# Gate and up in 128-token passes: four feature tiles to a PSUM tile instead of two, and the last 128 output rows cut 288 + 288 instead of 448 + 128

## The chip, the core and the metric

The kernel runs on one core of a Trainium2 chip. The metric is device time in microseconds (us) from start to end, lower is better. Single instructions are given in nanoseconds (ns). The engines are named as in the profile: PE (TensorE matmuls), PEld (its weight loads), DVE (VectorE), ACT (ScalarE), POOL (GpSimd) and SP (SyncE, which here only issues DMAs).

## What is computed

A transformer block of 2048 tokens with 576 features: a modulated layer norm, local attention in 32 heads (each token looks at itself and seven earlier tokens, two apart), a second modulated layer norm, and a gated MLP without a nonlinearity. All arrays are bfloat16. Cut to what matters:

```python
h = _layernorm(x) * (1 + ca) + sa
x = x + ga * attention(h, A_wqkv, A_wo)        # 8 keys per query, dilation 2
h = _layernorm(x) * (1 + cb) + sb
g = h @ w_gate                                  # 576 -> 4608
u = h @ w_up                                    # 576 -> 4608
x = x + gb * ((g * u) @ w_down)                 # 4608 -> 576
```

The six modulation rows come from `silu(c) @ w_mod`.

## The kernel before

**Chunks and passes.** The tokens are cut into ten chunks (`SIZES`, L34): four of 128 and six of 256. Attention works chunk by chunk (`project` and `attend`). Gate and up work in seven passes (`DOWN`, L36): four passes of 128 tokens (one chunk each), then three of 512 tokens (two chunks each). After the four 128-token passes, and after each 512-token pass, `down` multiplies 512 tokens by `w_down`.

**One pass of `gate_up` (L648).** The 4608 features are 36 tiles of 128, held as nine blocks of four (`FB`, L37). For each feature tile and each of gate and up there are five matmuls over the 576 input features: four *mains* with 128 rows (L679) and one *remainder* with the last 64 rows (L688). The gate remainder uses rows 0 to 63 of the array, the up remainder rows 64 to 127. A *unit* is what one PSUM tile of two banks holds: bank 0 is gate, bank 1 is up. In a 128-token pass a unit has two feature tiles (`nf`, L664), in a 512-token pass one. Three units make a group (`nu`, L705; there are three such PSUM tiles, `ps_mlp`, L101). A group runs in this order on PE: mains of unit 0, mains of unit 1, remainders of all three units in one burst, mains of unit 2. `evacuate` (L691) then has ACT copy a unit from PSUM to a bfloat16 tile `gu` (L697), and DVE multiply gate by up into `hh` (L701). There are two `gu` buffers. The PSUM of a unit is free for the next group when its ACT copy is done.

**What fills the time beside it.** Between the matmuls a `Pacer` (L775) runs the attention steps of the following chunk and the projection of the one after it, each at a fixed fraction of the pass. For the steps below: `turn` (L408) transposes the normalized tokens `xn` on PE; `modulate` (L427) writes `hT` from the two PSUM tiles turnA (three k-tiles, by DVE, L434) and turnB (two, by ACT, L436); `qk` (L472) multiplies `hT` by the query and key weights (`pq`, L485); the softmax subtracts on DVE (`dd`, L573), takes the exponential on ACT (L574), and DVE weights the shifted values (L611 to L614) into `o_sb`, which PE turns again and ACT copies to `oT` (L621, L622). Then come the output projection (`pw`, L628), the residual on DVE (`y`, L633), the second layer norm, and the value projection (`pv`, L510) with its ACT copies to `v_sb` (L514). The attention tiles share two PSUM banks (`ps_att`, L100).

**Order of the work.** Every engine runs its own instructions in order. For the four 128-token passes and their `down` the framework's scheduler decides that order from the program and its own estimates (`AUTO`, L38, L863). For the later passes PE keeps the program's order.

**Weights.** Blocks 2 to 5 stay in the space of `w_down` during the 128-token passes (`KEPT`, L46). The others go through three slots (`gwp`, L95). `block_done` (L333) asks for the next block's load when a block has been used: on POOL's queue in the first pass, later on SP's. Before the change it is called at the end of a group.

**The last rows.** `down` (L724) works through 128 tokens at a time with 36 matmuls for each of two halves of 288 columns, multiplies by `gb` (L742), adds the residual (L744) and stores. The last 128 rows are done in two parts, one after the other: 448 columns, then 128, each with its own store on SP.

Of the kernel before, what the change touches and what calls it, by code (L numbers as in the profile page):

```python
# [7 lines left out]
BF = mybir.dt.bfloat16  # L8
# [9 lines left out]
P = 128  # L18
D = 576
# [17 lines left out]
FB = 4  # L37
AUTO = 4  # L38
GU_BUFS = 3
NB = FT // FB  # L40

ORDER = [[0, 1, 2, 3, 4, 5, 6, 7, 8], [6, 7, 8, 5, 4, 3, 2, 1, 0], [8, 1, 0, 5, 4, 3, 2, 6, 7],
         [2, 0, 3, 6, 4, 5, 7, 1, 8], [7, 1, 8, 0, 2, 3, 4, 5, 6], [4, 5, 6, 0, 1, 2, 3, 7, 8],
         [3, 7, 8, 0, 1, 2, 4, 5, 6]]
# [19 lines left out]
def kernel(  # L64
# [13 lines left out]
    nc = tc.nc  # L78
    S = A_x.shape[1]
# [6 lines left out]
    def pool(name, bufs, **kw):  # L86
        return ctx.enter_context(tc.tile_pool(name=name, bufs=bufs, **kw))
# [11 lines left out]
    outp = pool("outp", 2)  # L99
# [3 lines left out]
    def att(shape, dt, name):  # L103
        return ps_att.tile(shape, dt, name=name, tag="att")

    def hp():
        return tc.high_priority()
# [11 lines left out]
    for sl, m0, off in ((slice(0, KT), 0, 0), (slice(KT, KT + 1), KT - 1, -64)):  # L119
        n = sl.stop - sl.start  # L120
# [10 lines left out]
    wd = wts.tile([P, FT, D], BF, name="wd")  # L131
# [18 lines left out]
    def load_x(ci, eng, js=None, behind=None):  # L150

        for j in range(SIZES[ci] // P) if js is None else js:
            xt = xin.tile([P, D], BF, name="x_t")
            if behind is not None:
                nc.vector.tensor_copy(xt[0:1, 0:1], behind)
            eng.dma_start(xt[:], x_flat[START[ci] + j * P:START[ci] + (j + 1) * P, :])
            x_tiles.setdefault(ci, []).append(xt)
# [167 lines left out]
    def load_next(ts=(0, 1), eng=nc.sync):  # L325
        if state["next"] < len(loads):
            load_gu(loads[state["next"]], ts, eng)
            state["next"] += 1

    def load_wd(f0, f1):  # L330
        nc.sync.dma_start(wd[:, f0:f1, :], B_w_down[f0 * P:f1 * P, :].rearrange("(k p) n -> p k n", p=P))

    def block_done(pi, b):  # L333
        if pi == KEPT_PASSES - 1 and b in KEPT:
            k = KEPT.index(b)
            load_wd(k * WDB, (k + 1) * WDB)
        for n in range(len(loads)):
            if last_use[n] == (pi, b) and n + GU_BUFS == state["next"]:
                load_next(eng=nc.gpsimd if pi == 0 else nc.sync)
        if (pi, b) == (0, ORDER[0][-2]):  # L340

            for cx in (4, 5):
                load_x(cx, nc.sync, behind=late["hh"][0:1, b * FB, 0:1])
            f0 = len(KEPT) * WDB
            nc.vector.tensor_copy(wd[0:1, f0, 0:1], late["hh"][0:1, b * FB, 0:1])
            load_wd(f0, FT)
# [301 lines left out]
    def gate_up(pi, c0, C, h2, step):  # L648

        hh = late["hh"]
        cs = slice(c0, c0 + C)
        ns = C / 2.4

        def tokens(rows, kt):
            return h2[rows, :, kt, :] if C > CH else h2[rows, c0 // CH, kt, c0 % CH:c0 % CH + C]

        def by_half(ap):  # L660
            return ap.rearrange("p (a c) -> p a c", c=CH) if C > CH else ap


        nf = 2 if C <= 256 else 1  # L664
        units = [(b, i) for b in ORDER[pi] for i in range(0, FB, nf)]

        def psum(k):

            if k < 3:
                t = ps_mlp.tile([P, 2, nf, 512 // nf], F32, name="pgu", tag="mlp")  # L670
                return [t[:, 0], t[:, 1]], t
            return [att([P, nf, 512 // nf], F32, "pgu" + "gu"[t])[:] for t in range(2)], None

        def main(u, first, beside=False):
            (b, i), out = units[u], ps[u][0]
            for n in range(nf):
                for t in range(2):
                    for kt in range(KT - 1):
                        nc.tensor.matmul(by_half(out[t][:, n, 0:C]), lhsT=gu_blocks[b][0][:, kt, t, (i + n) * P:(i + n + 1) * P], rhs=tokens(slice(0, P), kt),  # L679
                                         start=(first and n == 0 and kt == 0), stop=(not first and kt == KT - 2), skip_group_check=True)  # L680
                step(8 * ns, beside=beside if C > CH else None)

        def rem(u, first):
            (b, i), out = units[u], ps[u][0]
            for n in range(nf):
                for t in range(2):
                    rows = slice(64 * t, 64 * (t + 1))
                    nc.tensor.matmul(by_half(out[t][:, n, 0:C]), lhsT=gu_blocks[b][1][rows, (i + n) * P:(i + n + 1) * P], rhs=tokens(rows, KT - 1),  # L688
                                     start=(first and n == 0), stop=not first, skip_group_check=True)

        def evacuate(u):  # L691
            b, i = units[u]
            fs = slice(b * FB + i, b * FB + i + nf)
            with hp():
                g = late["gup"].tile([P, 2 * CM], BF, name="gu")[:, 0:2 * nf * C].rearrange("p (n t c) -> p n t c", n=nf, t=2)
                if ps[u][1] is not None:
                    nc.scalar.copy(g, ps[u][1][:, :, :, 0:C].rearrange("p t n c -> p n t c"))  # L697
                else:
                    for t in range(2):
                        nc.scalar.copy(g[:, :, t, :], ps[u][0][t][:, :, 0:C])  # L700
                nc.vector.tensor_tensor(hh[:, fs, cs], g[:, :, 0, :], g[:, :, 1, :], ALU.mult)  # L701

        nu = 4 if pi == len(passes) - 1 else 3  # L705
        ps, done = {}, 0
        for u in range(0, len(units), nu):
            for k in range(nu):
                ps[u + k] = psum(k)
                if k < 2:  # L710
                    main(u + k, True, k == 1)
            for k in range(nu):
                rem(u + k, k >= 2)
            step(2 * nu * nf * ns / 2)
            evacuate(u)
            evacuate(u + 1)
            for k in range(2, nu):
                main(u + k, False)
                evacuate(u + k)
            while done < NB and (done + 1) * FB <= (u + nu) * nf:  # L720
                block_done(pi, ORDER[pi][done])
                done += 1

    def down(di, r0, x_t, step):  # L724
        to_load = [(cx, j) for cx in LOAD_X_DOWN.get(di, []) for j in range(SIZES[cx] // P)]
        hh = late["hh"]
        for j in range(CM // P):

            cols = [(0, 448), (448, 128)] if r0 + (j + 1) * P == S else [(0, 288), (288, 288)]
            parts = [cols[0:1], cols[1:2]] if cols[0][1] != 288 else [cols]  # L730
            for part in parts:
                acc = ps_mlp.tile([P, 2, 512], F32, name="acc", tag="mlp")
                n, w, d0 = len(part), part[0][1], part[0][0]
                for f in range(FT):
                    for q, (q0, _) in enumerate(part):
                        nc.tensor.matmul(acc[:, q, 0:w], lhsT=hh[:, f, j * P:(j + 1) * P], rhs=wd[:, f, q0:q0 + w],  # L736
                                         start=(f == 0), stop=(f == FT - 1))
                    step(n * w / 2.4)
                with hp():
                    cs = slice(d0, d0 + n * w)  # L740
                    o_t = outp.tile([P, D], BF, name="y")[:, 0:n * w]
                    nc.vector.tensor_tensor(o_t.rearrange("p (n d) -> p n d", n=n), acc[:, 0:n, 0:w],  # L742
                                            gb_bc[:, cs].rearrange("p (n d) -> p n d", n=n), ALU.mult)
                    nc.vector.tensor_tensor(o_t, o_t, x_t[j][:, cs], ALU.add)  # L744
                (nc.gpsimd if n == 2 else nc.sync).dma_start(out_flat[r0 + j * P:r0 + (j + 1) * P, cs], o_t)  # L745
            if to_load:
                cx, jx = to_load.pop(0)
                load_x(cx, nc.gpsimd, [jx])
# [101 lines left out]
    def run_pass(pi):  # L850
        di, p = passes[pi]
        last = p is DOWN[di][-1]
        C = sum(SIZES[c] for c in p)
        total = FT * 9 * C / 2.4 + (FT * CM // P * 240 if last else 0)
        step = Pacer(passes[pi + 1][1] if pi + 1 < len(passes) else [], total)
        step(0)
        gate_up(pi, home[p[0]][1], C, h2T[di], step)
        if last:
            r0 = START[DOWN[di][0][0]]
            down(di, r0, [t for q in DOWN[di] for c in q for t in x_tiles[c]], step)  # L860
        step(0, rest=True)
# [36 lines left out]
```

## Time and profile before

| what | value |
|---|---|
| median of 4 runs | 574.71 us (574.07 to 575.86) |
| the profiled execution | 574.73 us, span 573.0 us |
| granted TensorE clock | 1.00 |
| four 128-token passes of gate and up, with the attention work beside them | 35.4 to 155.0 us of the span |
| last `down` of 512 rows | 534.1 us to the end |

The span goes from the first instruction to the last in the profile, and 1.7 us of the execution lie outside it. "Busy" is the time in which at least one instruction of the engine is open. PE's matmuls overlap in time, so PE counts as busy also where its matmuls start later than they could; such places show in the start times of neighbouring matmuls. In the views below a group of instructions is given as line, engine, operation, written tile <- read tiles, shape, count.

### The profile page before, as it was taken

The page shows a single profiled execution, that of the slowest core. Times are in us where ns is not written, and L with a number is a line of the kernel's source. Part 1 is how long each engine was busy: PE and PEld are TensorE (multiplying, and loading weights), DVE is VectorE, ACT ScalarE, POOL GpSimd, SP SyncE. Part 2 cuts the span into 40 slices and gives each one's busy share as a digit, 9 for nine tenths or more (in the row PEclk, how much of TensorE's full clock was granted, in tenths as well). Part 3 has the DMA queues.
Part 4 walks back from the last instruction along what each step waited for, and adds up shares of the span by engine and source line. Part 5 has one row for each costly group of instructions (what it writes and reads, how often), then busy time and mean ns, then how long its engine had stood idle before and what let it go on. Part 6 is the DMA issues. An engine that isn't in the chain of part 4 may idle for free.

```text
span 573.0 us, 12242 instructions
## 1 busy us (share of the span) xinstructions
PE 561.9 (98%) x5171; PEld 368.4 (64%) x5171; DVE 317.9 (55%) x695; ACT 222.2 (39%) x395; POOL 94.3 (16%) x165
## 2 busy tenths in 40 slices
PE   8899999999999999999999999999999999999997
PEld 4578898988878764554468764554457754444674
DVE  5778696868788775655394535744374422222201
ACT  3455565555602225445442005454440025444200
POOL 5462202020213211020501240011200110000000
PEclk9999999999999999999999999999999999999999
DMA  9999765259750345468402633476202214540000
GB/s 287 281 355 339 261 199 179 84 182 330 238 184 27 105 154 166 124 213 202 131 1 78 220 92 97 125 254 217 82 1 57 68 39 147 166 156 1 1 22 21
DMA packets 68457, 84.32 MB, mean 147 GB/s; under 512 B 19746, under 2 KB 59506, under 8 KB 68402
## 3 DMA queue, kind: packets, MB, share of 16 engines
q1 hardware_dynamic: 56738, 45.86, 27.2%
q0 software_dynamic: 9104, 34.44, 17.9%
q10 hardware_dynamic: 2560, 3.25, 1.7%
q8 instruction: 40, 0.66, 0.5%
q14 instruction: 15, 0.12, 0.1%
HBM read 70.93 MB, written 8.67 MB: 139 GB/s over the span
## 4 chain that ended last, share of the span: by engine, by line
PE 86%; DMA 8%; DVE 3%; ACT 1%; issue 1%; POOL 0%; ACTq 0%; DVEq 0%
PE pgu L679 38%; PE acc L736 24%; PE pgu L688 6%; PE pq L485 5%; DMA wd<-in_B_w_up_dram 4%; DMA wm<-in_w_mod_dram 4%; PE lgT L553 2%; PE pwB L628 2%; PE pwA L628 1%; PE pguu L679 1%; PE pgug L679 1%; PE pvA L510 1%; PE pvB L510 1%; PE warm L275 1%; DVE ln_stats L377 1%
## 5 line engine op out<-in xcount | busy, mean ns | idle before, releaser
L679 PE MATMUL pgu<-h2T,gm 128*128 128x512 bf16 (+1 forms) x1432 | 223.1, 308 | 1.1 <-ACT gu L697 0.7
L679 PEld LDWEIGHTS <-gm 128*128 128x128 bf16 x1504 | 119.0, 98 | 107.7 <-issue 14.2
L697 ACT CAST gu<-pgu 128x1024 bf16<-128x1024 f32 (+1 forms) x171 | 136.7, 835 | 130.1 <-PE pgu L688 103.6
L736 PE MATMUL acc<-wd,hh 128*128 128x288 bf16 (+2 forms) x1152 | 146.4, 286 | 0.0
L701 DVE TENSOR_TENSOR hh<-gu 128x512 bf16<-128x512 bf16 (+1 forms) x180 | 65.7, 370 | 127.6 <-ACT gu L697 118.5
L736 PEld LDWEIGHTS <-hh 128*128 128x128 bf16 x1152 | 110.9, 98 | 30.3 <-issue 0.4
L544 DVE TENSOR_TENSOR prod<-qT,kT 128x1280 bf16<-128x1280 bf16 (+1 forms) x80 | 47.0, 636 | 13.7 <-PE lgT L553 12.5
L527 POOL DMA_DIRECT2D vsh<-vd x30 | 22.7, 761 | 154.5 <-DMA vd<-v_sb 114.7
L745 POOL DMA_DIRECT2D out_dram<-y x15 | 8.5, 565 | 214.3 <-DVE y L744 214.3
L485 PE MATMUL pq<-hT,wqk 128*128 128x256 bf16 (+1 forms) x400 | 41.2, 251 | 0.8 <-DMA wqk<-in_A_wqkv_dram 0.8
L742 DVE TENSOR_TENSOR y<-acc,gb_bc 128x576 bf16<-128x576 f32 (+2 forms) x17 | 12.2, 718 | 51.8 <-PE acc L736 51.8
L611 DVE TENSOR_TENSOR vsh<-vsh,attn 128x2304 bf16<-128x2304 bf16 x30 | 39.9, 1352 | 0.2
L485 PEld LDWEIGHTS <-wqk 128*128 128x128 bf16 x400 | 32.3, 98 | 6.8 <-DMA wqk<-in_A_wqkv_dram 1.5
L679 PE MATMUL pgu<-h2T,wd 128*128 128x128 bf16 x512 | 34.9, 219 | 1.0 <-DMA wd<-in_B_w_up_dram 1.0
L688 PE MATMUL pgu<-h2T,gr 64*128 64x512 bf16 (+1 forms) x358 | 34.5, 307 | 0.0
L679 PEld LDWEIGHTS <-wd 128*128 128x128 bf16 x512 | 30.1, 98 | 2.9 <-DMA wd<-in_B_w_up_dram 1.5
L383 ACT ACTIVATE ln_rstd<-ln_stats,eps 128x2 f32<-128x2 f32 (+1 forms) x20 | 5.9, 296 | 66.4 <-DVE ln_stats L378 66.4
L377 DVE BATCH_NORM_STATS2 ln_stats<-x_t 128x6 f32<-128x288 bf16 x64 | 26.2, 447 | 1.8 <-DMA x_t<-in_A_x_dram 1.1
L688 PEld LDWEIGHTS <-gr 64*128 64x128 bf16 x376 | 12.5, 94 | 17.5 <-issue 10.6
L633 DVE TENSOR_TENSOR y<-pwA,ga_bc 128x288 bf16<-128x288 f32 x15 | 6.8, 456 | 26.1 <-PE pwA L628 25.9
L612 DVE TENSOR_TENSOR vsh<-vsh 128x2304 bf16<-128x2304 bf16 x15 | 20.3, 1352 | 0.0
L425 POOL TENSOR_SCALAR h2T<-h2T,modc 128x256 bf16<-128x256 bf16 x25 | 14.9, 604 | 30.0 <-DMA h2T<-xn_d 30.0
(153 smaller groups left out, 492.2 us busy)
## 6 DMA issues: line engine op xcount, KB each, us to landing
vsh<-vd POOLq DMA_DIRECT2D x30, 576.0 KB, 6.3
gm<-in_B_w_gate_dram SPq DMA_DIRECT2D x24, 512.0 KB, 3.9
gm<-in_B_w_up_dram SPq DMA_DIRECT2D x24, 512.0 KB, 5.0
wd<-in_B_w_down_dram SPq DMA_DIRECT2D x4, 1152.0 KB, 8.2
gm<-in_B_w_gate_dram POOLq DMA_DIRECT2D x5, 512.0 KB, 11.9
gm<-in_B_w_up_dram POOLq DMA_DIRECT2D x5, 512.0 KB, 11.7
out_dram<-y POOLq DMA_DIRECT2D x15, 144.0 KB, 2.1
wd<-in_B_w_gate_dram POOLq DMA_DIRECT2D x4, 512.0 KB, 10.1
```

The costliest lines, as they stand in the source:

```text
L377: nc.vector.bn_stats(stats[:, j, hf, :], src[j][:, hf * 288:(hf + 1) * 288])
L485: nc.tensor.matmul(pq[:, gi, 0:C], lhsT=wqk[:, kt, w0:w0 + P], rhs=h[:, kt, :], start=(kt == 0), stop=(kt == KT - 1))
L527: nc.gpsimd.dma_start(vsh[:].rearrange("p w d h -> p w (d h)"), src)
L544: nc.vector.tensor_tensor(prod[:, 0:nm, 0:C], qT[:, 0:nm, 0:C], kT[:, 0:nm, off:off + C], ALU.mult)
L611: nc.vector.tensor_tensor(vsh[:], vsh[:], attn[:, j, ws, None, :].to_broadcast([P, WG, DH, H]), ALU.mult)
L612: nc.vector.tensor_tensor(va[:], va[:], vb[:], ALU.add)
L628: nc.tensor.matmul(pw[q][:, 0:288], lhsT=oT[:, m, j * P:(j + 1) * P], rhs=wo[:, m, q * 288:(q + 1) * 288], start=(m == 0), stop=(m == KT - 1))
L679: nc.tensor.matmul(by_half(out[t][:, n, 0:C]), lhsT=gu_blocks[b][0][:, kt, t, (i + n) * P:(i + n + 1) * P], rhs=tokens(slice(0, P), kt), s ...
L688: nc.tensor.matmul(by_half(out[t][:, n, 0:C]), lhsT=gu_blocks[b][1][rows, (i + n) * P:(i + n + 1) * P], rhs=tokens(rows, KT - 1), start=(f ...
L697: nc.scalar.copy(g, ps[u][1][:, :, :, 0:C].rearrange("p t n c -> p n t c"))
L701: nc.vector.tensor_tensor(hh[:, fs, cs], g[:, :, 0, :], g[:, :, 1, :], ALU.mult)
L736: nc.tensor.matmul(acc[:, q, 0:w], lhsT=hh[:, f, j * P:(j + 1) * P], rhs=wd[:, f, q0:q0 + w], start=(f == 0), stop=(f == FT - 1))
```

## The change

In a 128-token pass a unit now has four feature tiles, one whole block: the two PSUM banks are filled to all 512 columns. A pass has 9 units in 3 groups instead of 18 in 6. `block_done` moves into the group, behind the evacuation of each unit after the first. And the last 128 rows are cut as 288 and 288 columns, still one part after the other. In the passes of 512 tokens a unit stays as it was.

```diff
-        nf = 2 if C <= 256 else 1
+        nf = min(FB, 512 // C)
...
             step(2 * nu * nf * ns / 2)
-            evacuate(u)
-            evacuate(u + 1)
-            for k in range(2, nu):
-                main(u + k, False)
+            for k in range(nu):
+                if k >= 2:
+                    main(u + k, False)
                 evacuate(u + k)
-            while done < NB and (done + 1) * FB <= (u + nu) * nf:
-                block_done(pi, ORDER[pi][done])
-                done += 1
+                while k > 0 and done < NB and (done + 1) * FB <= (u + k + 1) * nf:
+                    block_done(pi, ORDER[pi][done])
+                    done += 1
...
-            cols = [(0, 448), (448, 128)] if r0 + (j + 1) * P == S else [(0, 288), (288, 288)]
-            parts = [cols[0:1], cols[1:2]] if cols[0][1] != 288 else [cols]
-            for part in parts:
+            halves = [[0], [1]] if r0 + (j + 1) * P == S else [[0, 1]]
+            for qs in halves:
                 acc = ps_mlp.tile([P, 2, 512], F32, name="acc", tag="mlp")
...
```

The scheduler makes a new order of the four 128-token passes from it, on PE, ACT and DVE. On POOL the order stays. On SP a few weight loads change places. Behind these passes all queues keep their order.

More of the change, by code (lines that the diff above doesn't have):

```diff
@@ L727, in down @@
         for j in range(CM // P):
-            cols = [(0, 448), (448, 128)] if r0 + (j + 1) * P == S else [(0, 288), (288, 288)]
-            parts = [cols[0:1], cols[1:2]] if cols[0][1] != 288 else [cols]
-            for part in parts:
+            halves = [[0], [1]] if r0 + (j + 1) * P == S else [[0, 1]]
+            for qs in halves:
                 acc = ps_mlp.tile([P, 2, 512], F32, name="acc", tag="mlp")
-                n, w, d0 = len(part), part[0][1], part[0][0]
                 for f in range(FT):
-                    for q, (q0, _) in enumerate(part):
-                        nc.tensor.matmul(acc[:, q, 0:w], lhsT=hh[:, f, j * P:(j + 1) * P], rhs=wd[:, f, q0:q0 + w],
+                    for q in qs:
+                        nc.tensor.matmul(acc[:, q, 0:288], lhsT=hh[:, f, j * P:(j + 1) * P], rhs=wd[:, f, q * 288:(q + 1) * 288],
                                          start=(f == 0), stop=(f == FT - 1))
-                    step(n * w / 2.4)
+                    step(120 * len(qs))
                 with hp():
-                    cs = slice(d0, d0 + n * w)
-                    o_t = outp.tile([P, D], BF, name="y")[:, 0:n * w]
-                    nc.vector.tensor_tensor(o_t.rearrange("p (n d) -> p n d", n=n), acc[:, 0:n, 0:w],
+                    n, cs = len(qs), slice(qs[0] * 288, (qs[-1] + 1) * 288)
+                    o_t = outp.tile([P, D], BF, name="y")[:, 0:n * 288]
+                    nc.vector.tensor_tensor(o_t.rearrange("p (n d) -> p n d", n=n), acc[:, qs[0]:qs[-1] + 1, 0:288],
                                             gb_bc[:, cs].rearrange("p (n d) -> p n d", n=n), ALU.mult)
```

## The prediction

> **What bounds the kernel now.** I read the page first, then the chain of waits, then the timeline of the four 128-token passes, because only these passes and the last 128 rows change.
>
> ```profile
> PE 561.9 (98%) x5171; PEld 368.4 (64%) x5171; DVE 317.9 (55%) x695; ACT 222.2 (39%) x395; POOL 94.3 (16%) x165
> ...
> PE 86%; DMA 8%; DVE 3%; ACT 1%; issue 1%; POOL 0%; ACTq 0%; DVEq 0%
> ```
>
> PE is the bound, at full granted clock. Only two things can help: fewer or shorter steps of PE, and fewer places where PE's next matmul starts late. The table by stage gives PE 86.00 busy of 86.00 us from 207 to 293 us and likewise in the later passes, whose order stays as it is. So the change is worth what it does between 35 and 155 us, plus the tail.
>
> ```profile
> 31.33 9.21 DMA wd<-in_B_w_up_dram
> 40.83 13.12 DMA wd<-in_B_w_up_dram
> 53.99 0.84 PE pgu L679 x12
> ```
>
> These rows of the chain (start, length, what) show the first pass waiting for weights: block 5's up half lands at 40.83 + 13.12 = 53.95, and PE starts on it then. What PE saves before 53.95 is lost in this wait.
>
> ```profile
> 67.24 0.62 PE L679 MATMUL pgu<-h2T,gm 128*128 128x128 bf16 x8
> 67.79 0.51 PE L688 MATMUL pgu<-h2T,gr 64*128 64x128 bf16 x12
> ...
> 68.12 1.07 ACT L697 CAST gu<-pgu 128x512 bf16<-128x512 f32 x2 [1.99 <-PE pgu L688]
> 68.23 0.62 PE L679 MATMUL pgu<-h2T,gm 128*128 128x128 bf16 x8
> ```
>
> This is one burst of remainders. Mains follow each other at 56 ns (a row of 32 takes 1.79 us from start to start). Eight mains from 67.24 would end at 67.69, but the burst starts at 67.79. The twelve remainders are six gate-up pairs at 56 ns, 0.34 us, and would end at 68.13, but the next main starts at 68.23. So each burst costs 0.19 us beyond its matmuls. The first copy starts 0.33 us into the burst.
>
> **The change part by part.**
>
> 1. *Fewer bursts.* Matmuls and their lengths stay. Six bursts per pass become three. In passes 1 to 3 (counting from 0) nine bursts go: 9 x 0.19 = 1.7 us. In pass 0, after 53.95, three bursts become one, and twelve remainders that stood behind the wait now stand ahead of it, where PE has 0.7 us to spare: 2 x 0.19 + 0.34 = 0.7 us. **Sum -2.4 us.** The start times show 92 to 96 ns a side at every burst, so I hold this within 0.3.
>
>    The Trainium skill, "TensorE: Matmul & The Clock Gate", Part 3, The mechanism, says that a weight load overlaps a running matmul only when the two use different row groups. By that rule the load between two mains would be exposed as well and a burst would cost nothing extra; this term would be 0 and my sum 576.0. The rows above disagree: mains with 98 ns loads run at 56 ns, and only the change of row count costs.
>
> 2. *Old waits that go.* They are read from start times. Pass 1: turnB comes 0.34 late, because its PSUM bank is held until `dd` is done; mains at 89.49 come 0.61 late, since the unit's copy only ends then. Pass 2: the same two, 0.18 and 0.44. Pass 3: 0.31 for turnB and 0.20 for products. In the new order 24 remainders and 8 mains stand between the logits and the transposes instead of 16 mains (in pass 3 it is DVE's maximum that no longer queues behind a multiply), and the copy has 32 mains (1.79 us) to hide in instead of 16. **Sum -2.1 us**, bounds -1.0 and -2.1.
>
> 3. *New waits.* The copy becomes one of 1024 columns. Its length is in the passes of 512 tokens:
>
> ```profile
> L697 ACT CAST gu<-pgu 128x1024 bf16<-128x1024 f32 x99 | 96.9, 1015 | 107.6 <-PE pgu L688 87.3 <-PE pgu L679 8.6 <-DVE hh L701 6.2
> L697 ACT CAST gu<-pgu 128x512 bf16<-128x512 f32 x72 | 39.8, 588 | 22.6 <-PE pgu L688 16.3 <-DVE hh L701 3.0 <-PE pgu L679 1.6
> ```
>
>    Two copies of 588 become one of 1015: 36 x 0.161 = 5.8 us less of ACT, and DVE's multiply likewise (2 x 286 to 425 ns: 5.3 us less). Neither sets the end, so this is worth nothing by itself. But where a copy stands matters more. Now:
>
> ```profile
> 71.16 0.33 PE L414 MATMUL turnA<-identw,xn 128*128 128x128 bf16 x3
> ...
> 71.65 0.42 ACT L574 ACTIVATE dd<-dd 128x256 f32<-128x256 f32 x1 [1.15 <-DVE dd L573]
> ...
> 71.99 0.81 ACT L436 ACTIVATE hT<-turnB,modc 128x128 bf16<-128x128 bf16 x2
> ...
> 72.72 1.07 ACT L697 CAST gu<-pgu 128x512 bf16<-128x512 f32 x2
> ```
>
>    The exponential and ACT's half of `hT` come ahead of the two copies, and `pq` at 73.23 finds `hT` ready (72.80). In the new order ACT has: copy, copy, exponential, `hT`. Counted from the burst's start: the first copy waits for eight remainders instead of four, so 0.33 + 2 x 0.056 = 0.45. Two copies take about 0.91 each before the next can start, so the exponential starts at 2.27 and `hT` ends 1.15 later (71.65 to 72.80 above): 3.4. PE meanwhile needs 0.77 for the burst, 0.45 for 8 mains, 0.28 for five transposes, 1.0 for 18 mains: `pq` begins at 2.5 and needs ACT's k-tiles from 2.7. It loses **0.7 us** in pass 1. In pass 2 DVE writes its three k-tiles of `hT` (1.04 us) only behind the second multiply (2.4 + 0.4 = 2.8), so they are complete at 3.84: **0.8 us**. In pass 0 the same wait falls before 53.95 and costs nothing. In pass 3 the scheduler put the third copy there, with 24 mains to cover it: nothing.
>
>    Behind these stands the attention chain, later by some 0.9 us: in pass 1 `o_sb`, which had 0.4 us to spare (79.46 against 79.86), and the two banks of `pv` cost 0.1 each. In pass 2 DVE gets two multiplies of 0.4 instead of one of 0.2 between the products and `y`, so `pv`'s banks come free 0.46 late, the second `pv` and the transpose behind it wait 0.3 and 0.75 instead of 0.18 and 0.43: 0.9 more. In pass 3 the copies to `oT` stand behind a copy of twice the size: 0.4 more. **Sum +3.1 us** (0.9 + 1.7 + 0.5). Below, this is 0, if ACT's backlog is shorter than I add up; above I take twice it, 6 us, since the trace does not show this order.
>
>    A rule of the skill speaks against the change: "Perfetto Trace Analysis", Optimizing Scalar/DVE Operations, says that engines which are not saturated but cause bubbles elsewhere may do better with instructions broken up. ACT is 56% busy from 100 to 158 us, so the rule would have this term decide; without it the sum would be that of the first rival.
>
> 4. *Weights.* A group is three whole blocks, so without the moved `block_done` a slot would come back later. With it, a load waits for the mains of its block, as now. In pass 0 block 8's up half lands at 62.84, and PE needs it at 63.0 in the new order: 0.2 us of cover; if that is gone, the loss is as large as the lateness. Later loads land 5 us or more before use. 0, up to +0.5.
>
> 5. *The tail.* PE's time is equal: 36 x 189 + 36 x 56 = 8.8 us, and 72 x 122.5 = 8.8 us. What follows the last matmul grows:
>
> ```profile
> 567.58 0.62 DVE L742 TENSOR_TENSOR y<-acc,gb_bc 128x448 bf16<-128x448 f32 x1 [5.56 <-PE acc L736]
> 568.24 0.39 DVE L744 TENSOR_TENSOR y<-y,x_t 128x448 bf16<-128x448 bf16 x1
> ...
> 569.59 0.29 DVE L742 TENSOR_TENSOR y<-acc,gb_bc 128x128 bf16<-128x128 f32 x1 [0.96 <-PE acc L736]
> 569.91 0.23 DVE L744 TENSOR_TENSOR y<-y,x_t 128x128 bf16<-128x128 bf16 x1
> ```
>
>    Halfway between 128 and 448 columns lie 0.46 and 0.31: +0.17 and +0.08, and the last store is larger. **+0.3 us**, bounds +0.2 and +0.6.
>
> **Sum.** The profiled execution took 574.73 us (span 573.0 and 1.7 around it), the median is 574.71, so no shift between them. 574.73 - 2.4 - 2.1 + 3.1 + 0.3 = **573.6 us**.
>
> **Rivals.** About 0.3%, or 1.7 us, is what a measurement of this kernel can tell from no change: faster ends at 573.0, slower begins at 576.4.
>
> *The new waits don't come* (term 3 near 0). For it: ACT and DVE have 11 us less to do and PE has more cover per copy. Against it: the order on ACT is fixed, and two copies stand ahead of the exponential. 574.73 - 2.4 - 2.1 + 0.3 = 570.5 us. Chance 0.22.
>
> *The attention chain sets the pace of passes 1 to 3.* Its place is ACT between burst and exponential, its price the lateness of `hT`, `o_sb`, `y` and `v_sb` in turn. The chain has 0.4 us to spare at `o_sb`; beyond that each 0.1 us shows. With 0.9 at `hT`, 0.8 at `y` and 0.5 at `v_sb` a pass loses 2.2: 3 x 2.2 - 2.4 - 2.1 + 0.3 = +2.4, so 577.1 us. It decides from 1.4 us a pass (4.2 / 3). Against it: in pass 3 the third copy lies clear of the exponential. Chance 0.13.
>
> *The forecast*, 572.2 to 575.2 by itself: chance 0.65. A quarter of it lies below 573.0.
>
> Faster: 0.22 + 0.15 = 0.37. Slower: 0.13 and 0.02 of the forecast's upper end, 0.15. Same: 0.48. The range leaves out about one in ten on each side: 571.0 to 576.2.
>
> **What would show it.** Right: three bursts per pass on PE in the timeline, and 12 fewer of them; two copies of about 1.0 us ahead of the exponential; `pq` broken by a wait of 0.7 to 0.8 us in passes 1 and 2; the mains after a burst never late by ACT; the last multiply near 0.46 us. Wrong: `pq` without a gap (first rival), or `o_sb`, `pw` and `pv` waiting in every pass by 0.5 us or more (second), or mains of blocks 7 and 8 waiting for DMA.

## The result, and the profile after

The changed kernel takes **575.72 us** (median of 40 runs, 574.82 to 578.06); the kernel before took 574.92 beside it (58 runs). The ratio is 1.0015, 95% interval 1.0010 to 1.0020: 0.8 us slower, inside the forecast's range, but on the wrong side of no change. The profiled execution took 575.73 us, with a span of 574.0 at a granted clock of 0.998.

From the page of the changed kernel, the busy times, the shares of the chain that ended last, and ACT's copy:

```profile
PE 558.2 (97%) x5171; PEld 370.0 (64%) x5171; DVE 315.9 (55%) x659; ACT 217.3 (38%) x359; POOL 93.4 (16%) x165
...
PE 86%; DVE 5%; DMA 4%; ACT 2%; issue 1%; SPq 0%; POOL 0%; ACTq 0%; POOLq 0%; DVEq 0%
...
L697 ACT CAST gu<-pgu 128x1024 bf16<-128x1024 f32 x135 | 132.2, 1017 | 122.2 <-PE pgu L688 100.2
```

The change did what it says: 36 instructions fewer on ACT and on DVE, all copies are of 1024 columns, the same 5171 matmuls, and PE is busy 3.7 us less. The span is 1.0 us longer all the same, so PE must stand still for longer than it saved. Where, is read from the start times of the same places in PE's program (us; pass 3 runs up to the end of the first output projection `pw` behind it):

| stretch | before | after | difference | forecast |
|---|---|---|---|---|
| pass 0, together with its start | 65.34 | 64.91 | -0.43 | -0.7 |
| pass 1 | 27.37 | 27.05 | -0.32 | -0.6 |
| pass 2 | 31.58 | 31.60 | +0.02 | +0.5 |
| **pass 3** | **36.51** | **38.08** | **+1.57** | **-0.6** |
| rest of the first `down` | 46.79 | 46.55 | -0.24 | 0 |
| the 512-token passes and their `down` | 361.96 | 361.97 | 0 | 0 |
| last matmul to the end | 3.44 | 3.81 | +0.37 | +0.3 |

One row is wrong in kind: pass 3. First the place that came as forecast, in the timeline of the changed kernel in pass 1 (start, length, engine, line, what, and in brackets the idle time before it and who ended it):

```profile
69.89 0.84 PE L688 MATMUL pgu<-h2T,gr 64*128 64x128 bf16 x24
...
70.33 1.93 ACT L697 CAST gu<-pgu 128x1024 bf16<-128x1024 f32 x2 [1.07 <-PE pgu L688]
...
70.67 0.62 PE L679 MATMUL pgu<-h2T,gm 128*128 128x128 bf16 x8
71.12 0.33 PE L414 MATMUL turnA<-identw,xn 128*128 128x128 bf16 x3
...
72.14 0.43 ACT L574 ACTIVATE dd<-dd 128x256 f32<-128x256 f32 x1
...
72.46 0.81 ACT L436 ACTIVATE hT<-turnB,modc 128x128 bf16<-128x128 bf16 x2
...
73.32 0.27 PE L485 MATMUL pq<-hT,wqk 128*128 128x128 bf16 x2 [0.75 <-ACT hT L436]
```

ACT does two long copies, then the exponential, then `hT`; `pq` comes 0.91 us late by its start time. The end of pass 3 in the same kernel:

```profile
146.90 1.50 PE L679 MATMUL pgu<-h2T,gm 128*128 128x128 bf16 x24
...
147.71 0.33 ACTq L517 DMA_DIRECT2D vd<-v_sb  x1
...
150.34 1.96 PE L679 MATMUL pgu<-h2T,gm 128*128 128x128 bf16 x32
153.16 0.40 ACT L514 CAST v_sb<-pvA 128x288 bf16<-128x288 f32 x1 [5.49 <-DMA vd<-v_sb]
...
153.61 0.49 PE L414 MATMUL turnA<-identw,o_sb 128*128 128x128 bf16 x6 [1.31 <-ACT v_sb L514]
...
154.65 1.96 ACT L697 CAST gu<-pgu 128x1024 bf16<-128x1024 f32 x2
...
154.83 1.63 PE L733 MATMUL acc<-wd,hh 128*128 128x288 bf16 x12 [0.50 <-ACT gu L697]
...
156.46 0.86 ACT L621 COPY oT<-turnA 128x768 bf16<-128x768 bf16 x1
...
157.37 0.30 PE L628 MATMUL pwA<-wo,oT 128*128 128x288 bf16 x1 [0.91 <-ACT oT L621]
```

A chunk of 256 tokens makes `v` in two halves. Each is copied by ACT from the banks `pvA`, `pvB` into `v_sb` and stored from there, and there is one `v_sb` (L140). So the copies of the second half must wait until the store of the first has landed. ACT stands still for 5.49 us. `turnA` needs the bank that these copies free: 32 mains from 150.34 at 56 ns end at 152.13, and it starts at 153.61, 1.48 us late. In ACT's order the last copies of `gu` and the copies to `oT` stand behind, so the first `acc` is 0.66 late and the two first `pw` 1.07 and 0.36 (0.36 on `pwB` was there before). The chain of waits says it in one piece (start, length, what):

```profile
147.27 0.41 ACT v_sb L514
147.71 5.38 DMA vd<-v_sb
153.46 0.41 ACT v_sb L514
153.86 0.36 ACT gu L697
```

In the kernel before the same wait was there, and it was covered:

```profile
149.88 0.33 ACTq L517 DMA_DIRECT2D vd<-v_sb  x1
...
153.03 0.40 ACT L514 CAST v_sb<-pvA 128x288 bf16<-128x288 f32 x1 [1.84 <-DMA vd<-v_sb]
...
154.41 0.50 PE L414 MATMUL turnA<-identw,o_sb 128*128 128x128 bf16 x6
```

`pvA` was free at 153.03 + 0.40 = 153.43, and `turnA` came at 154.41: 0.98 us of cover. The changed kernel arrives at 152.13, 2.28 us earlier, while the store lands 0.13 later. 2.28 - 0.98 + 0.13 = 1.43 of the 1.48 us. Counted from the start of pass 3, where 0.72 us of earlier gains drop out, the sum is the same: `turnA` is due 1.56 us earlier and the store lands 0.85 later, although it is issued 1.4 us earlier. Beside it run two loads of `w_down` of 1152 KB each, on SP. They are issued at 140.85 and 142.00 in the changed kernel (before at 142.85 and 144.06) and land at 150.11 and 153.61 (before at 149.31 and 152.53).

### The profile page after: what moved, and what is told of

It reads as the page before. It is cut to its first block, busy times and chain, and to the rows that moved or that the text cites. A ratio compares the mean times of both kernels' runs of the same rounds, so it can differ in the third digit from the quotient of the medians.

```text
span 574.0 us, 12135 instructions
## 1 busy us (share of the span) xinstructions
PE 558.2 (97%) x5171; PEld 370.0 (64%) x5171; DVE 315.9 (55%) x659; ACT 217.3 (38%) x359; POOL 93.4 (16%) x165
## 4 chain that ended last, share of the span: by engine, by line
PE 86%; DVE 5%; DMA 4%; ACT 2%; issue 1%; SPq 0%; POOL 0%; ACTq 0%; POOLq 0%; DVEq 0%
PE pgu L679 38%; PE acc L733 24%; PE pgu L688 5%; PE pq L485 5%; PE lgT L553 2%; DMA wv<-in_A_wqkv_dram 2%; DMA wqk<-in_A_wqkv_dram 2%; PE pwB L628 2%; PE pwA L628 1%; PE pguu L679 1%; PE pgug L679 1%; PE pvA L510 1%; PE pvB L510 1%; DMA vd<-v_sb 1%; DVE vsh L611 1%
## 5 line engine op out<-in xcount | busy, mean ns | idle before, releaser
L697 ACT CAST gu<-pgu 128x1024 bf16<-128x1024 f32 x135 | 132.2, 1017 | 122.2 <-PE pgu L688 100.2
L733 PE MATMUL acc<-wd,hh 128*128 128x288 bf16 x1152 | 146.4, 286 | 0.5 <-ACT gu L697 0.5
L733 PEld LDWEIGHTS <-hh 128*128 128x128 bf16 x1152 | 112.4, 98 | 29.4 <-issue 1.0
L701 DVE TENSOR_TENSOR hh<-gu 128x512 bf16<-128x512 bf16 x144 | 60.8, 425 | 127.3 <-ACT gu L697 118.5
L739 DVE TENSOR_TENSOR y<-acc,gb_bc 128x576 bf16<-128x576 f32 (+1 forms) x17 | 12.2, 717 | 52.0 <-PE acc L733 52.0
L688 PE MATMUL pgu<-h2T,gr 64*128 64x512 bf16 (+1 forms) x358 | 33.1, 307 | 0.0
L383 ACT ACTIVATE ln_rstd<-ln_stats,eps 128x2 f32<-128x2 f32 (+1 forms) x20 | 5.9, 296 | 67.3 <-DVE ln_stats L378 67.3
L628 PE MATMUL pwA<-wo,oT 128*128 128x288 bf16 x75 | 19.0, 286 | 0.9 <-ACT oT L621 0.9
```

The lines of the kernel that those rows point to most:

```text
L628: nc.tensor.matmul(pw[q][:, 0:288], lhsT=oT[:, m, j * P:(j + 1) * P], rhs=wo[:, m, q * 288:(q + 1) * 288], start=(m == 0), stop=(m == KT - 1))
L733: nc.tensor.matmul(acc[:, q, 0:288], lhsT=hh[:, f, j * P:(j + 1) * P], rhs=wd[:, f, q * 288:(q + 1) * 288], start=(f == 0), stop=(f == FT ...
```

## The experiments

**Theories.** T1: pass 3 loses because one `v_sb` ties ACT, and all that is queued behind it, to the landing of a store. T2: the copies of doubled length on ACT do the harm everywhere, and `v_sb` only shows it. T3: the store is that slow because of the loads of `w_down` beside it. T3 can hold together with T1. All ratios below are to the kernel before, run beside them. Two profiled executions (two `v_sb`, 574.30 us, and the last row of the table, 573.33 us) began pass 0 some 2 to 3.5 us later than the rest, for reasons in the setup that I did not follow; so the traces are compared by the lengths of the stretches from pass 1 on. Passes 1 and 2 repeat within 0.01 us between profiles of kernels with the same program there; pass 3 repeats within 0.25 us (36.51 before and 36.28 in the kernel of experiment 9, whose pass 3 is that of the kernel before).

| kernel | median, us | ratio, 95% interval | pass 1 | pass 2 | pass 3 |
|---|---|---|---|---|---|
| before | 574.92 | 1 | 27.37 | 31.58 | 36.51 |
| after | 575.72 | 1.0015 (1.0010-1.0020) | 27.05 | 31.60 | 38.08 |
| after, two `v_sb` | 571.79 | 0.9954 (0.9939-0.9970) | 27.05 | 31.02 | 34.82 |
| after, only `attn` moved | 575.67 | 1.0010 (1.0001-1.0019) | 27.05 | 31.60 | 38.00 |
| before, two `v_sb` | 574.14 | 0.9985 (0.9976-0.9993) | 27.36 | 31.57 | 36.07 |
| after, pass 3 old | 574.72 | 1.0003 (0.9992-1.0013) | 27.05 | 31.61 | 36.56 |
| after, two `wd` loads left out | 571.89 | 0.9952 (0.9940-0.9964) | 27.06 | 31.60 | 34.81 |
| after, q later | 575.46 | 1.0012 (1.0001-1.0024) | 27.05 | 31.21 | 38.44 |
| two `v_sb`, copies split | 572.34 | 0.9953 (0.9940-0.9965) | 27.64 | 31.08 | 35.00 |
| two `v_sb`, exponential first, q later | 571.13 | 0.9935 (0.9919-0.9950) | 26.87 | 30.82 | 34.81 |

**1. Two buffers of `v_sb`.**

```diff
-    v_sb = once.tile([P, D], BF, name="v_sb")
+    vsbp = pool("vsbp", 2)
...
-                vt = v0 if ci == 0 else v_sb
+                vt = v0 if ci == 0 else vsbp.tile([P, D], BF, name="v_sb")
...
-        attn = small.tile([P, CH // P, W, H], BF, name="attn", bufs=1)[:, 0:ST]
+        attn = lgs[:].rearrange("p g c -> p (g c)")[:, 0:ST * W * H].rearrange("p (j w h) -> p j w h", j=ST, w=W)
```

> The changed kernel with v_sb in two buffers (attn shares the memory of lgs, to make room); nothing is left out. T1 (pass 3 loses because ACT, with one v_sb, stands still until the store of the first half has landed, and the last copies of gu and of oT are queued behind it): the waits of 1.48 us (turnA behind the copy of v_sb), 0.66 us (first down matmul behind the copy of gu) and half or more of the 1.43 us (pw behind oT) go, 2.1 to 2.9 us below the changed kernel, so 572.8 to 573.6 us, 1.3 to 2.1 below the kernel before. T2 (the copies of doubled size load ACT, and v_sb only shows it): at most 0.5 us below the changed kernel, 575.2 or more. In the trace T1 wants no idle of ACT behind the store.

571.79 us, 3.9 below the changed kernel: more than T1 asked for, and T2 is out as the cause of the loss, though the long copies do cost something in passes 1 and 2 (`pq` is 0.91 late here too). The timeline at the end of pass 3:

```profile
149.64 0.33 ACTq L517 DMA_DIRECT2D vd<-v_sb  x1
...
151.77 0.41 ACT L514 CAST v_sb<-pvB 128x288 bf16<-128x288 f32 x1
152.06 1.03 ACT L697 CAST gu<-pgu 128x1024 bf16<-128x1024 f32 x1
...
154.07 0.50 PE L414 MATMUL turnA<-identw,o_sb 128*128 128x128 bf16 x6
```

The second half is copied as soon as its products are done, the copies of `gu` follow, and `turnA` has no wait (32 mains from 152.27 end at 154.06). The first store still takes 5.24 us, but ACT no longer waits for it. Pass 3 is 3.26 us shorter than in the changed kernel, which is the 1.48 + 0.66 + 1.07 of the late starts, and 1.69 us shorter than in the kernel before. Pass 2, which also makes two halves of `v`, is 0.58 shorter; together that is 3.84 of the 3.9 us. In pass 2 it is not the landing of the store (118.43 in the changed kernel), but the order on ACT that decides. In the changed kernel the second half stands behind a layer norm's `L383`, which waits for DVE:

```profile
118.96 0.30 ACT L383 ACTIVATE ln_rstd<-ln_stats,eps 128x2 f32<-128x2 f32 x1 [2.31 <-DVE ln_stats L378]
119.17 0.38 ACT L514 CAST v_sb<-pvA 128x288 bf16<-128x288 f32 x1
```

With two buffers the scheduler puts the copies ahead of it:

```profile
120.40 0.40 ACT L514 CAST v_sb<-pvA 128x288 bf16<-128x288 f32 x1 [1.23 <-PE pvA L510]
...
121.48 0.30 ACT L383 ACTIVATE ln_rstd<-ln_stats,eps 128x2 f32<-128x2 f32 x1 [0.38 <-DVE ln_stats L378]
```

In pass 3 ACT's order is the same in both kernels.

**2. The part that made room, alone.** Only the last of the three edits above.

> The changed kernel with one v_sb, as it is, and only attn put into the memory of lgs: the part of the two-buffer version that was there to make room. T1 (the second buffer alone does it): as the changed kernel, 575.3 to 576.2 us, with the wait of turnA behind v_sb at the end of pass 3 at about 1.5 us. If the sharing does any of it: 573.5 us or less.

575.67 us, with `turnA` 1.40 late and pass 3 at 38.00. The second buffer does it, not the place of `attn`.

**3. The same two buffers in the kernel before.**

> The kernel before the change with v_sb in two buffers (attn shares the memory of lgs, as in the changed kernel with two). T1 (the second buffer is worth what TensorE waits behind v_sb): in the profile of before, turnA 0.29, turnB 0.14, pv 0.18 and a main matmul 0.44 us at the end of pass 2 stand behind ACT's copies, and in pass 3 nothing does: 0.3 to 1.0 us below before, 573.9 to 574.6 us, pass 2 shorter, pass 3 as it was. If two buffers help in some other way (the 3.8 us that they took off the changed kernel have nothing to do with the change), 2.5 us or more below before: 572.4 us or less.

574.14 us, ratio 0.9985: T1's size. Pass 2 did not get shorter, against my expectation: its waits at the banks of `pv` stayed (turnA 0.29 late, the main 0.44), because ACT's copies there stand behind the layer norm's `L383`, as in the kernel before. Pass 3 with `pw` is 0.44 shorter, though that length differs by 0.23 between profiles of the same program (36.51 and 36.28, experiment 9). So the store cost the old kernel less than half a microsecond there and the changed one 3.3. Between the two kernels with two buffers, the change is worth -0.31% (0.9954 against 0.9985; the intervals do not overlap), or 2.1 us less in passes 1 to 3 by the table.

**4. Pass 3 as it was.** Passes 0 to 2 and the tail are new.

```diff
-        nf = min(FB, 512 // C)
+        nf = 2 if C <= 256 and pi == 3 else min(FB, 512 // C)
```

> The changed kernel with two feature tiles to a PSUM tile in pass 3 alone, as before the change; passes 0 to 2 and the tail are new. If the loss is made in pass 3 (T1), 1.3 to 2.1 us below the changed kernel: 573.6 to 574.4 us, with the waits at the end of pass 3 as in the kernel before. If it comes from the larger copies in every pass (T2), pass 3 gives back a fourth of it, no more than 0.5 us: 575.2 or more.

574.72 us, a little above T1's span, with pass 3 back at 36.56 (before 36.51). The loss is made in pass 3. Passes 1 and 2, with long copies, are 0.32 shorter and 0.03 longer than before.

**5. Without the last two loads of `w_down`.**

```diff
-        if pi == KEPT_PASSES - 1 and b in KEPT:
+        if pi == KEPT_PASSES - 1 and b in KEPT[:2]:
```

> The changed kernel without the last two loads of wd of 1152 KB that stand beside the end of pass 3 (a part of wd is left as it was, so the last products use other weights; the work on the engines is the same). T3 (the loads slow the store of v, 5.37 us against 1.75 us of other stores): the store lands in 1.8 to 3.1 us, ACT's second pair of copies is done before turnA is due, 1.5 to 2.9 us below the changed kernel, 572.8 to 574.2 us. T1 without T3 (the store is slow for another reason, or any store is long enough): the store still takes about 5 us and the time stays within 0.4 us of the changed kernel, 575.3 to 576.1 us.

571.89 us, below what T3 asked for (572.8 to 574.2). Pass 3 takes 34.81, the same as with two buffers. This kernel leaves out a part of the weights, so its output is another one. The timeline:

```profile
148.06 0.33 ACTq L517 DMA_DIRECT2D vd<-v_sb  x1
...
149.89 0.40 ACT L514 CAST v_sb<-pvA 128x288 bf16<-128x288 f32 x1 [1.86 <-PE pvA L510]
```

ACT's second pair now waits for the products of `pv`, not for the store, which landed after 1.75 us. With the loads beside it the same store took 5.38. Pass 2 stays at 31.60: of the 3.8 us, pass 3 is 3.27 and the tail 0.36. So the loss needs both, the single buffer and the loads: taking away either brings pass 3 to 34.8.

**6. The `pq` wait: q due later.**

```diff
-AT_FIRST = dict(AT, hT=.24, q0=.29, q1=.34,
+AT_FIRST = dict(AT, hT=.24, q0=.33, q1=.36,
```

> The changed kernel with the first q product of a chunk due later (q0 .29 to .33, q1 .34 to .36), which puts 18 main matmuls, about 1.0 us, ahead of it in passes 0 to 2. T1 with the wait of pq as a term of its own (0.90 to 0.91 us in each of the three passes): 0.8 less in passes 1 and 2, 0 to 0.8 in pass 0, pass 3 keeps its loss: 1.6 to 2.4 us below the changed kernel, 573.3 to 574.1 us. T2 (ACT as a whole is behind by the long copies): the wait moves to the next thing that needs ACT, at most 0.5 us gained, 575.2 or more.

575.46 us: too little for the first expectation. Its premise was off: 24 mains instead of 18 stand ahead of the first `pq`, 6 more and not 18, or 0.34 us. The wait fell by 0.33, from 0.91 to 0.58 us. In pass 1 the gain went straight into the next wait:

```profile
73.34 0.72 PE L485 MATMUL pq<-hT,wqk 128*128 128x128 bf16 x10 [0.42 <-ACT hT L436]
...
80.06 0.34 PE L414 MATMUL turnA<-identw,o_sb 128*128 128x128 bf16 x3 [0.47 <-DVE o_sb L614]
```

By start times `turnA` is 0.63 late instead of 0.30, and pass 1 takes 27.05 us as before. Here DVE sets the pace, as the traces read: in this kernel it works from 71.39, when the first copy of `gu` is done, to the end of `o_sb` at 80.00 with no gap over 0.04 us (in the changed kernel from 71.37 to 79.97). It is DVE's whole list up to `o_sb`, multiplies of gate and up among it, and not the exponential, that `turnA` waits for. Counted from the start of pass 1, `o_sb` ends at 15.06 in both. Pass 2 gained 0.39, and pass 3, where `turnA` still waits for the store, was 0.36 longer.

**7. Each long copy split in two** (on top of two buffers).

```diff
-                    nc.scalar.copy(g, ps[u][1][:, :, :, 0:C].rearrange("p t n c -> p n t c"))
+                    for n0 in range(0, nf, 2):
+                        n2 = slice(n0, min(nf, n0 + 2))
+                        nc.scalar.copy(g[:, n2], ps[u][1][:, :, n2, 0:C].rearrange("p t n c -> p n t c"))
```

> The changed kernel with two buffers of v_sb and with each copy of four feature tiles split into two copies of 512 columns. ACT's order becomes four short copies, hT, exponential. T1 (what is left of the new waits is ACT's order behind the burst, pq 0.90 to 0.91 in passes 0 to 2): hT comes ahead of the exponential (0.43 us) and the copies cost more in sum, so pq waits 0.5 to 0.9 us and o_sb more: within 0.6 us of the version with two buffers, 571.2 to 572.4 us. T2 (the length of one copy does the harm): 1.0 to 2.0 us below the version with two buffers, 569.8 to 570.8 us.

572.34 us, not faster than with whole copies. In pass 1:

```profile
70.06 2.05 ACT L699 CAST gu<-pgu 128x512 bf16<-128x512 f32 x4 [1.07 <-PE pgu L688]
...
71.97 0.84 ACT L436 ACTIVATE hT<-turnB,modc 128x128 bf16<-128x128 bf16 x2
72.67 0.45 ACT L574 ACTIVATE dd<-dd 128x256 f32<-128x256 f32 x1
...
80.33 0.34 PE L414 MATMUL turnA<-identw,o_sb 128*128 128x128 bf16 x3 [0.77 <-DVE o_sb L614]
```

Four short copies take 2.05 us, two long ones 1.93. The order behind them only swaps `hT` and the exponential: `pq` is 0.84 late and `o_sb` 0.93, so pass 1 is 0.59 longer. `pq` could not come earlier by ACT alone. DVE's last k-tile of `hT` stands behind a multiply that was not split and ends at 72.83, as ACT's half does at 72.81:

```profile
72.14 0.43 DVE L703 TENSOR_TENSOR hh<-gu 128x512 bf16<-128x512 bf16 x1
72.49 0.34 DVE L434 TENSOR_SCALAR hT<-turnA,modc 128x128 bf16<-128x128 bf16 x1
```

And the later exponential makes DVE wait 0.33 us for it. The Trainium skill, "Perfetto Trace Analysis", Optimizing Scalar/DVE Operations, says that breaking up instructions may help where an engine that is not saturated makes bubbles on others; here shorter pieces on ACT alone did not help, since what stands behind which on ACT and DVE stayed.

**8. The exponential first, and q later** (on top of two buffers; `q0`, `q1` as in 6).

```diff
-        nc.scalar.activation(dd, dd, ACTF.Exp, scale=scale)
+        with hp():
+            nc.scalar.activation(dd, dd, ACTF.Exp, scale=scale)
```

> The changed kernel with two buffers of v_sb, the exponential in high priority (ACT's order: copy, exponential, copy, hT) and the q products due later (q0 .33, q1 .36; in the trace that puts 24 instead of 18 main matmuls ahead of the first of them). Later q alone cut the wait of pq from 0.91 to 0.58 us, but o_sb then came 0.63 instead of 0.30 us late in pass 1. If the attention chain behind the exponential sets the end of passes 0 to 2, an exponential 1.0 us earlier takes the wait of o_sb away and the later q counts: 0.6 us in pass 1, 0.3 to 0.6 in pass 2, 0 to 0.6 in pass 0, so 0.9 to 1.8 us below the version with two buffers, 570.0 to 570.9 us. If something else on ACT or DVE is next, 0.4 us or less: 571.4 us or more.

571.13 us, but run on another occasion than the plain two buffers, and the intervals overlap. The traces give 0.18 and 0.20 us in passes 1 and 2. `o_sb` still comes 0.43 late, so the exponential on ACT was not the main thing that held it. The trace shows DVE at work without a gap over 0.04 us from its first multiply to the end of `o_sb`, 8.42 us (8.60 with two buffers alone):

```profile
73.30 0.43 DVE L702 TENSOR_TENSOR hh<-gu 128x512 bf16<-128x512 bf16 x1 [0.49 <-ACT gu L698]
...
81.26 0.46 DVE L615 TENSOR_TENSOR o_sb<-vsh 128x576 bf16<-128x576 bf16 x1
```

`o_sb` ends 0.18 us earlier in the pass than with two buffers alone, and pass 1 is 0.18 shorter. In experiment 7 both are later, by 0.56 and 0.59. So pass 1 follows the end of `o_sb`. Less work on DVE ahead of `o_sb` should shorten it; no run here tries that.

**9. The tail alone, in the kernel before** (288 and 288 columns there).

> The kernel before the change with the last 128 rows as 288 and 288 columns, nothing else. The products behind the last matmul take 0.77 us for 288 columns instead of 0.52 for 128: 0.25 us more at the end, 575.1 us, within the scatter of the runs; its trace should show the stretch from the last matmul to the last product 0.25 us longer and the rest unchanged. If the transfer of the last columns counts as well (144 columns more per row), 0.4 us or more.

575.18 us, ratio 1.0005 (0.9995 to 1.0015): nothing that a time shows. Its trace has 3.82 us from the last matmul to the end instead of 3.44: 0.38 more, so the transfer counts as well (288 - 128 is 160 columns more per row, not 144).

**10 and 11. The best version.** Two buffers with the old columns at the end, without and with the edits of 8.

> The changed kernel with two buffers of v_sb and with the last 128 rows as 448 and 128 columns again. From the last matmul to the end the traces show 3.44 us with the old columns and 3.81 to 3.84 with the new in the kernels that compute the reference: 0.37 us below the version with two buffers, which gave 571.79: 571.4 us. If the old columns' extra matmul time shows (no such stretch was seen), 571.8 us.

> The same as the one beside it (two buffers of v_sb, old columns at the end) and also the exponential in high priority and q due later (q0 .33, q1 .36). The traces of passes 1 and 2 gave 0.38 us for these two, pass 0 was covered by setup and loads: 0.4 to 0.7 us below the one beside it, 570.7 to 571.0 us. If they gain nothing once the waits of pass 0 are counted, the same as the one beside it.

571.35 us, ratio 0.9955 (0.9937 to 0.9972), and 571.59 us, ratio 0.9942 (0.9930 to 0.9954). Side by side the edits of 8 are worth nothing that can be told. The old columns show 3.45 us behind the last matmul in both. Passes 1 to 3 of the first take 27.05, 31.02 and 34.81 us, as in experiment 1. Both versions beat the kernel before by about 3 us, and that comes from the second buffer of `v_sb` together with the four-tile units.

## Why the prediction was wrong, step by step

1. *Fewer bursts, -2.4: right in passes 1 to 3.* The switches between 128 and 64 rows show as starts that are late by 93 to 96 ns, one into and one out of each burst. In each of these passes there are 12 before and 6 after, and their sum falls from 3.45 to 1.72 us: 1.73, where 1.7 was forecast. The trace goes on speaking against the rule weighed there, by which a burst would cost nothing extra. But "only the change of row count costs" was too narrow: the products `lgT`, with 128 rows and 32 columns of weights, also start 93 ns late behind a main (at 66.34 and 68.25 in the changed kernel). What pass 0 gained can't be told: from its first main it takes 28.70 us in the changed kernel, but 29.59 and 29.80 in those of experiments 4 and 5, whose program is the same there. The prediction counted on PE waiting for weights at 53.95. In the profile of the changed kernel pass 0 begins 0.84 us later than before, and its weights are there in time: the waits for loads, 1.71 us in sum before, are gone. So that -0.43 is near the forecast -0.7 is partly chance.

2. *Old waits that go, -2.1: right.* None of the listed waits is left: 0.95 us in pass 1, 0.62 in pass 2, 0.51 in pass 3.

3. *New waits, +3.1: the step that failed, in pass 3.* Pass 1 lost 1.21 for 0.9 (`pq` 0.91 for 0.7, `o_sb` 0.30 for 0.1). Pass 2 lost 1.2 for 1.7: `pq` was 0.90 for 0.8, but `pv` and the transposes only 0.3 more, for 0.9. **Pass 3 lost 3.2 for 0.5.** I priced the copies to `oT` behind one longer copy, 0.4. I did not ask what else stands in ACT's order there, though the trace of before showed it: ACT idle 1.84 us behind a store, with 0.98 us of cover at `turnA`. The steps ahead of it took that cover away. The step that failed is thus this wait for the landing of the store, which the sum put at nothing. The whole term was 5.6 us, just inside its upper bound of 6. That bound was the estimate doubled; that the time lies within the stated range comes from this margin and not from a mechanism that had been seen. The signs listed as "right" came true (three bursts, two long copies ahead of the exponential, a gap at `pq`, the last multiply at 0.46 us) while the time went up, since none of them looks at the end of pass 3.

4. *Weights, 0: right in this profile.* No main matmul waits for a load in it. Profiles of other variants show such waits in pass 0, up to 2.1 us in sum; the kernel before has 1.7.

5. *Tail, +0.3: right*, with 0.37. The timeline at the end:

```profile
566.63 4.77 SPq L742 DMA_DIRECT2D out_dram<-y  x2
570.21 0.46 DVE L739 TENSOR_TENSOR y<-acc,gb_bc 128x288 bf16<-128x288 f32 x1 [3.61 <-PE acc L733]
570.70 0.31 DVE L741 TENSOR_TENSOR y<-y,x_t 128x288 bf16<-128x288 bf16 x1
```

   The two products take 0.46 and 0.31, as read between the shapes, 0.25 more than for 128 columns. The other 0.12 is the last store: from the last product to the end 2.98 us instead of 2.85. The kernel of experiment 5, with the new columns, has 2.61 there and ended after 3.45 us; why its last store was quicker stays open.

The sum with the measured terms of passes 1 to 3 is -1.7 - 2.1 + 5.6 = 1.8 where the table has 1.27. The difference is in pass 3: its products `lgT` are 0.6 us shorter in sum than before, of which the list has 0.2, and the first `pw` was 0.08 late before. The *first rival* (the new waits don't come) was wrong, though with two buffers the kernel comes within 1.3 us of its 570.5. The *second rival* named the right engine and tile, `v_sb` on ACT, but as 0.5 us in each of three passes and through ACT's own work. It was one place, 3.2 us, and a DMA. In pass 1 its chain does set the pace (experiments 6 to 8), but by the work on DVE and not by ACT, and at a length that is still below the old one.

Left open: what pass 0 is worth, and why the last store in experiment 5 was quicker.

## What to carry to other kernels

Before a change is credited with making PE earlier, look at every point where another engine waits for a DMA, even where nothing is late today, and subtract the cover there from the gain: what PE gains beyond it comes back as a wait. A tile with one buffer that is stored and rewritten ties its engine, and all that is queued behind it in that engine's order, to the landing of the store. Here a second buffer turned a change that lost 0.8 us into one that wins about 3. In a program whose order a scheduler makes, look also at what the new buffer does to that order: 0.58 of the 3.9 us came from there.

## What the runs showed of the hardware

- A store of 144 KB landed after 1.75 us with nothing beside it (experiment 5) and after 5.38 us beside two loads of 1152 KB, although it was issued on ACT's queue and the loads on SP's. Issued 2.2 us earlier than in the kernel before (147.71 for 149.88), it let ACT go on at nearly the same time (153.16 for 153.03): the last load landed at 153.61 for 152.53, so issuing the store earlier bought nothing. The Trainium skill, "DMA: Bandwidth & Descriptors", Issuing engines are not separate DMA queues, says that such transfers run on the same DMA engines and interleave; the run without the loads agrees.
- Copies from PSUM on ACT follow each other faster than their length: two of 1024 columns (1.02 us each) took 1.93 us together, and four of 512 columns took 2.05.
